# First w_gate group by units and both, fourth attention unit in single bursts, third weight groups by halves: a fused sliding-window attention and gated feed-forward kernel

## The chip, the cores and the metric

The kernel runs on one core of one Trainium2 chip. The metric is device time in microseconds (us) of one launch, the median of several runs.

## The reference

Attention over 8 batches x 8 heads, 576 positions of 64 numbers each, where a position sees itself and the 63 before it; then a feed-forward layer over the 4608 tokens, 512 numbers wide inside and out, 1536 wide in the middle.

```python
q, k, v: (8, 8, 576, 64) float32
scores = matmul(q, k^T) / sqrt(64);   masked where not 0 <= i - j < 64
attn   = softmax(scores);             x = matmul(attn, v)  -> (4608, 512)
out    = (maximum(x @ w_gate, 0) * (x @ w_val)) @ w_out       # float32, (4608, 512)
w_gate, w_val: (512, 1536);  w_out: (1536, 512)
```

## The kernel before

The tokens are worked on in tiles: four of 384 tokens (tile 0 to 3) and six of 512. The attention of a 384-token tile is done in two *units* of 192 tokens; units 0 and 1 belong to tile 0, units 2 and 3 to tile 1, and so on. The types on chip are 16-bit floats with 32-bit sums.

One unit goes through these steps, each a function of the kernel: `u_st` (scores on TensorE, 24 small products for each half of the heads, called `hh` 0 and 1), `u_exp` (ScalarE), `u_mask` (VectorE), `u_pv` (values on TensorE, again 24 small products for each `hh`), `u_recip` and `u_norm` (VectorE; `u_norm_act` does one half on ScalarE with six copies), and `u_turn` (two VectorE transpositions that write the x tile `xt`, two of its four chunks of 128 for each `hh`). Before a batch's first scores, q and k are loaded by POOL's DMA queue into `nats` (`qk_load`, L179) and transposed on VectorE (`qk_trans`, L199, two for k and two for q); v is loaded by `v_load` (L205) and spread by `v_spread` (L215 on an engine, L217 by SP's DMA queue).

The feed-forward layer has 12 output columns blocks `f` of 128 in its middle. Tiles 0 and 1 are computed by `hidden` (L589): for groups of four f, the products with w_gate (four chunks c of the contraction each), `relu` on ScalarE (L572), the products with w_val, and the gate product on VectorE (L575) that writes `g_sb`. Then `output` multiplies by w_out (L1023), copies the result on ScalarE and stores it by SP's queue (L1036). Later tiles use `fast_hidden` (L634; the sums on VectorE are L670), `fast_output`, and for the last six `SevenOut` (L847), which form fewer, larger products with prepared sums of the weights (`w_form`, L528) and of x (`x_form`). Nothing of these is changed but one list, `SEVEN[-1]`.

The weights come in by POOL's queue in three groups of four f for each matrix, and each group in two halves `a` of two contraction chunks each (`w_load`, L159). The order on POOL's queue is: v of units 0 and 1, first w_gate and w_val group, second groups, v of unit 2, third groups, q and k of the next batch, v of unit 3, w_out.

The order of instructions on every engine is written out by the program when it is built: the `Weaver` holds a clock and a list of planned steps with due times. The feed-forward products advance the clock by their assumed length, and steps that fall due are issued between them (`W.at(T, ...)`, `W.advance`). `w_need` makes the clock wait for a weight group's assumed landing. On the chip, semaphores alone decide: each engine runs its instructions in this order, each as soon as its operands are there. PSUM has eight banks; `one_bank` goes round banks 0 to 3 for the feed-forward products of tiles 0 and 1, `two_banks` round 4 to 7 for the attention units.

Of the kernel before, what the change touches and what calls it, by code (L numbers as in the profile page):

```python
# [10 lines left out]
FP32 = mybir.dt.float32  # L11
FP16 = mybir.dt.float16
# [35 lines left out]
def kernel(  # L48
# [10 lines left out]
    nc = tc.nc  # L59
# [94 lines left out]
    def w_load(wt, src, f0, f1, landed):  # L154

        if wt is not wo:
            ns = slice(128 * f0, 128 * f1)
            for a in range(2):
                nc.gpsimd.dma_start(wt[:, 2 * a:2 * a + 2, ns], src.rearrange("(a p e) n -> a p e n", a=2, e=2)[a, :, :, ns])  # L159
        if wt is wo:  # L160
            nc.gpsimd.dma_start(wo[:, f0:f1], src.rearrange("(c p) n -> p c n", p=128)[:, f0:f1])
        w_done.update(((wt.name, f), landed) for f in range(f0, f1))

    def w_need(wt, f):
        while (wt.name, f) not in w_done:
            W.pop()
        W.advance(w_done[wt.name, f])

# [176 lines left out]
    def u_recip(u, hhs=(0, 1)):  # L345
        d = units[u]
        if "r" not in d:
            d["r"] = a_n.tile([128, 2, SB, 1], FP32, name="r")
        for hh in hhs:
            nc.vector.reciprocal(d["r"][:, hh], pv_of(d, u, hh)[:, :, D:D + 1])  # L350
# [21 lines left out]
    def u_turn(u, hhs=(0, 1)):  # L372

        d = units[u]
        c0 = U * (u % 2)
        h0, h1 = hhs[0], hhs[-1] + 1
        for hh in range(h0, h1):
            dst = xt_tile(u // 2)[:, 2 * hh:2 * hh + 2, c0:c0 + U].rearrange("p e (s c) -> p s e c", c=32)
            nc.vector.transpose(dst, d["x"][:, hh])
# [27 lines left out]
    def part_written(banks):  # L407
        written.update((id(to), 0) for to in banks)
# [129 lines left out]
    def plan_exps(T, u, mask=True, gap=0.4, first=0.8):  # L538
        for i in range(G):
            W.at(T + first + gap * i, lambda i=i: u_exp(u, i))  # L540
            if mask:
                W.at(T + first + 0.45 + gap * i, lambda i=i: u_mask(u, i))
# [11 lines left out]
        while normed[0] < n:  # L554
            W.pop()

    def hidden(t, spans, f0=0, f1=NF, each=1):

        if t not in gs:
            gs[t] = g_sb_p.tile([128, NF, WT], FP16, name="g_sb"), {}  # L560
        g_sb, done = gs[t]
        xt = xt_tile(t)
        n = spans[0][1] - spans[0][0]

        w = 512 // n
# [12 lines left out]
        for fb in range(f0, f1, each):  # L578
            r2s = [f_sb.tile([128, 2, WT], FP32, name="pr", bufs=4) for _ in range(2)]
            r_sbs = {}  # L580
            for i, wt in enumerate((wg, wv)):
                for c0, f in ((c0, f) for c0, _ in spans for f in range(fb, fb + each, w)):
                    h = one_bank()
                    part_written([h])
                    for b in range(w):
                        W.advance(W.clock)
                        w_need(wt, f + b)
                        for c in range(NC):
                            nc.tensor.matmul(h[:, b * n:b * n + n], wt[:, c, (f + b) * 128:(f + b) * 128 + 128],  # L589
                                             xt[:, c, c0:c0 + n], start=(c == 0), stop=(c == NC - 1))  # L590
                        W.clock += 4 * (n + 7) / 2400.0
                    if i == 0:
                        r_sb = r_sbs[c0, f] = r2s[len(r_sbs) // 2][:, len(r_sbs) % 2]
                        W.at(W.clock, lambda r_sb=r_sb, h=h: relu(r_sb, h))
                    else:
                        W.at(W.clock, lambda f=f, c0=c0, r_sb=r_sbs[c0, f], h=h: gate(f, c0, r_sb, h))

    def fast_hidden(t, seven=None):

# [467 lines left out]
    XAT = -0.3  # L1067
    SEVEN_LAST = (("P6", "P5", "P2", "P7", "oP1", "P3", "P4"), ("P6", "P5", "P2", "P7", "oP1", "P4", "P3"))
    SEVEN = {n: ("P2", "v0", "v1", "P6", "P5a", "P7", "s0", "P5b", "P4", "s1", "P3") for n in (-5, -4, -3, -2)}
    SEVEN[-1] = ("v0", "P2", "P6", "v1", "P5a", "P7", "P5b", "P4", "h1", "P3")  # L1070

    SEVEN[0] = ("P2", "P4", "P5", "P6", "P7", "P3")

    with tc.manual_schedule():
# [45 lines left out]
        for hh in range(2):  # L1120
            u_recip(0, (hh,))
            u_norm(0, hh)
        u_turn(0)
        for hh in range(2):
            u_pv(1, (hh,), True)
        heat(1, units[1]["st"][3])
        for hh in range(2):
            u_recip(1, (hh,))
        u_norm_act(1, 1)
        u_norm(1, 0)  # L1130
        for hh in range(2):
            u_turn(1, (hh,))
# [16 lines left out]
        for u in (4, 5):  # L1149
            v_load(u)  # L1150
        for i, (name, hh) in enumerate((n, hh) for n in "kq" for hh in range(2)):
            W.at(31.6 + 1.4 * i, lambda name=name, hh=hh: qk_trans(1, name, hh))
        for hh, T in enumerate((36.6, 38.8)):
            W.at(T, lambda hh=hh: u_st(3, (hh,)))
            for i in range(G):
                W.at(T + 0.4 + 0.22 * i, lambda hh=hh, i=i: u_exp(3, i, (hh,)))
                W.at(T + 0.8 + 0.22 * i, lambda hh=hh, i=i: u_mask(3, i, (hh,)))
            W.at(T + 3.5 - 0.7 * hh, lambda hh=hh: u_pv(3, (hh,)))
            W.at(T + 4.0 - 0.7 * hh, lambda hh=hh: u_recip(3, (hh,)))
            W.at(T + 4.1 - 0.7 * hh, lambda hh=hh: u_norm(3, hh))  # L1160
            W.at(T + 4.6 - 0.7 * hh, lambda hh=hh: u_turn(3, (hh,)))
        W.at(37.4, lambda: v_spread(3, pool))
        W.at(40.6, lambda: behind_masks(3))

        def pair(t, TA, TB, P):
            for u, T in ((2 * t, TA), (2 * t + 1, TB)):
# [53 lines left out]
        def ahead(t):  # L1220
            T = W.clock
            long = widths[t] == WT
            ends = T + (32.7 if long else 22.5)
            if t + 2 <= LAST:
                qk_turns(t + 2, T, LATE if t - 1 in FAST_OUT else (0.1, 1.4, 8.0, 14.2) if long else (0.1, 1.4, 6.1, 10.7) if t < NS - 1 else (2.4, 6.1, 10.7, 14.2))
                v_ahead(t + 2, ends, ends + VAT if t in FAST_OUT else ends - 5.0 if long else T + 3.0 if t == 2 else ends + 1.5)
# [8 lines left out]
        for T, gap, eng, some in ((40.5, 0.1, nc.gpsimd, sums[0][:4] + sums[1][:3]), (52.8, 0.1, nc.gpsimd, sums[1][3:8]),  # L1235
                                  (48.2, 0.6, nc.vector, sums[0][4:8]), (68.1, 0.1, nc.gpsimd, sums[0][8:]),
                                  (64.5, 0.7, nc.vector, sums[1][8:])):
            for i, (w, j, n) in enumerate(some):
                W.at(T + gap * i, lambda eng=eng, w=w, j=j, n=n: w_form(eng, (wg, wv)[w], n, j))
# [21 lines left out]
        while any(id(one) in unread for one in singles[:4]):  # L1261
# [73 lines left out]
```

## Time and profile before

| what | value |
|---|---|
| time, median of 3 runs | 301.93 us (301.9 to 302.15) |
| profiled execution: its own time | 302.04 us |
| its span | 300.3 us |
| TensorE busy | 289.6 us, 96% |
| VectorE busy | 251.7 us, 84% |
| ScalarE busy | 196.0 us, 65% |
| POOL busy | 201.7 us, 67% |
| granted TensorE clock | 1.0 throughout |

PE is the page's name for TensorE's matrix products, DVE for VectorE, ACT for ScalarE, POOL for GpSimd, SP for the engine that issues most stores. A row of the timeline gives the start, the time to the end of the last instruction, the engine, the line, the operation, the tiles written and read with their form, the count, and in brackets the idle time of the engine before the row with what ended it. Products that follow each other overlap, so the spacing of their starts, not the length of one, is what a product costs.

### The profile page before, as it was taken

What the parts mean: (1) busy time and instruction counts of PE and PEld (TensorE: products, weight loads), DVE (VectorE), ACT (ScalarE), POOL (GpSimd) and SP (SyncE); (2) the same over time, 40 slices, a digit from 0 to 9 for tenths busy, and PEclk for the clock granted to TensorE, in tenths of its full rate; (3) what the DMA queues carried; (4) which work ended last, traced back from release to release, by engine and by line L of the source; (5) the groups of instructions that cost most, each with busy time, mean ns of one, the idle gap of its engine ahead of it and who ended that gap; (6) DMA issues with size and microseconds to landing.
All of it is one profiled execution on the core that took longest, in us unless ns stands there. A gap on an engine that the chain in (4) does not pass through costs nothing.

```text
span 300.3 us, 11073 instructions
## 1 busy us (share of the span) xinstructions
PE 289.6 (96%) x4643; PEld 239.4 (80%) x4643; DVE 251.7 (84%) x517; ACT 196.0 (65%) x408; POOL 201.7 (67%) x241
## 2 busy tenths in 40 slices
PE   4899999999999999999999999999999999999994
PEld 2475877748957975888888888888888888888894
DVE  5947895997995999789999899989858985896584
ACT  3545336258848848885798579857985698538850
POOL 8767689868957893985957595759375617441750
PEclk9999999999999999999999999999999999999999
DMA  7999999979919636911399239922911210031013
GB/s 216 183 196 194 194 197 179 160 131 241 80 40 181 164 70 149 146 42 38 61 219 120 60 53 219 126 57 53 173 37 35 74 41 0 3 103 41 0 38 105
DMA packets 59506, 33.20 MB, mean 111 GB/s; under 512 B 39552, under 2 KB 53824, under 8 KB 59456
## 3 DMA queue, kind: packets, MB, share of 16 engines
q0 software_dynamic: 46688, 18.29, 52.3%
q1 hardware_dynamic: 12192, 13.75, 15.1%
q8 instruction: 36, 0.59, 0.8%
q10 hardware_dynamic: 576, 0.46, 0.5%
q14 instruction: 14, 0.11, 0.1%
HBM read 37.75 MB, written 9.44 MB: 157 GB/s over the span
## 4 chain that ended last, share of the span: by engine, by line
PE 87%; DMA 5%; POOL 4%; DVE 2%; issue 1%; DVEq 0%; POOLq 0%
PE bank L634 46%; PE bank L847 17%; PE bank L589 7%; PE bank L767 5%; PE bank L1023 5%; PE bank L265 3%; DMA wg<-in_moe_w_gate_dram 3%; PE bank L465 2%; DMA v<-in_v_dram 2%; POOL v L205 1%; PE bank L336 1%; POOL wg L159 1%; DVE g_sb L659 1%; DVE g_sb L797 0%; POOL wv L159 0%
## 5 line engine op out<-in xcount | busy, mean ns | idle before, releaser
L659 POOL TENSOR_TENSOR g_sb<-pr 128x512 f16<-128x512 f32 (+1 forms) x36 | 42.7, 1193 | 43.6 <-ACT pr L676 43.6
L670 DVE TENSOR_TENSOR pr<-bank,pr 128x512 f32<-128x512 f32 (+1 forms) x96 | 58.5, 649 | 3.6 <-PE bank L634 1.9
L653 ACT COPY pr<-bank 128x512 f32<-128x512 f32 (+1 forms) x96 | 49.1, 566 | 13.7 <-PE bank L634 13.5
L659 DVE TENSOR_TENSOR g_sb<-r,bank 128x512 f16<-128x512 f32 (+1 forms) x48 | 31.3, 652 | 23.8 <-ACT r L703 22.4
L847 PEld LDWEIGHTS <-g_sb 128*128 128x128 f16 x444 | 41.8, 98 | 5.2 <-issue 0.2
L634 PE MATMUL bank<-xc,vs 128*128 128x256 f16 (+1 forms) x288 | 41.3, 266 | 0.0
L634 PE MATMUL bank<-xc,us 128*128 128x256 f16 (+1 forms) x288 | 41.3, 266 | 0.0
L634 PEld LDWEIGHTS <-vs 128*128 128x128 f16 x384 | 36.5, 98 | 3.5
L634 PEld LDWEIGHTS <-us 128*128 128x128 f16 x384 | 36.5, 98 | 3.3
L205 POOL DMA_DIRECT2D v<-in_v_dram x41 | 34.7, 866 | 2.2 <-DMA nats<-in_q_dram 1.0
L676 ACT ACTIVATE pr<-pr 128x512 f32<-128x512 f32 (+1 forms) x48 | 29.3, 610 | 9.8 <-DVE pr L670 9.8
L703 ACT ACTIVATE r<-bank 128x512 f32<-128x512 f32 (+1 forms) x48 | 27.7, 577 | 4.8 <-PE bank L634 4.0
L634 PEld LDWEIGHTS <-wg 128*128 128x128 f16 x288 | 27.4, 98 | 3.2
L634 PEld LDWEIGHTS <-wv 128*128 128x128 f16 x288 | 27.4, 98 | 2.6
L634 PE MATMUL bank<-xt,wg 128*128 128x256 f16 (+1 forms) x192 | 27.5, 266 | 0.0
L634 PE MATMUL bank<-xt,wv 128*128 128x256 f16 (+1 forms) x192 | 27.5, 266 | 0.0
L797 POOL TENSOR_TENSOR g_sb<-g_sb,xus 128x512 f16<-128x512 f16 x24 | 27.1, 1148 | 0.0
L847 PE MATMUL bank<-wo,g_sb 128*128 128x256 f16 (+1 forms) x222 | 26.6, 270 | 0.0
L430 ACT ACTIVATE pw<-bank 128x512 f16<-128x512 f32 x48 | 25.3, 605 | 1.1 <-PE bank L265 0.7
L847 PE MATMUL bank<-wts,g_sb 128*128 128x256 f16 (+1 forms) x222 | 25.4, 270 | 0.2 <-DVE xw L484 0.2
L643 ACT COPY bank<-bank 128x512 f32<-128x512 f32 (+1 forms) x48 | 24.6, 553 | 0.0
L572 ACT ACTIVATE pr<-bank 128x384 f32<-128x384 f32 x24 | 11.9, 501 | 15.5 <-PE bank L589 12.5
(107 smaller groups left out, 559.8 us busy)
## 6 DMA issues: line engine op xcount, KB each, us to landing
out_dram<-o_sb SPq DMA_DIRECT2D x30, 256.0 KB, 3.1
nats<-in_k_dram POOLq DMA_DIRECT2D x15, 288.0 KB, 6.1
nats<-in_q_dram POOLq DMA_DIRECT2D x15, 288.0 KB, 8.0
v<-in_v_dram POOLq DMA_DIRECT2D x31, 128.0 KB, 8.2
v<-v SPq DMA_DIRECT2D x27, 66.0 KB, 2.7
v<-v SPq DMA_DIRECT2D x13, 132.0 KB, 2.5
wg<-in_moe_w_gate_dram POOLq DMA_DIRECT2D x6, 256.0 KB, 6.4
wv<-in_moe_w_val_dram POOLq DMA_DIRECT2D x6, 256.0 KB, 8.1
```

Of the source, the lines that this page charges most:

```text
L205: nc.gpsimd.dma_start(v16s[b % 2][lo:hi, g, :, 0:64], v[b, :, 64 * g - 64 + lo:64 * g - 64 + hi].rearrange("h p d -> p h d"))
L430: nc.scalar.activation(d["p"][g].rearrange("p n c -> p (n c)"), d["st"][g], ACT.Exp, scale=scale)
L589: nc.tensor.matmul(h[:, b * n:b * n + n], wt[:, c, (f + b) * 128:(f + b) * 128 + 128], xt[:, c, c0:c0 + n], start=(c == 0), stop=(c == NC ...
L634: nc.tensor.matmul(to[:, HT * m:HT * m + HT], w[:, k, 128 * m:128 * m + 128], x[:, k], start=(first and m == 0 and k == 0), stop=(k == 1), ...
L643: nc.scalar.copy(at[j, "B", i][:, 0:TW], at[j, "A", i][:, 0:TW])
L653: nc.scalar.copy(pr[:, i], at[j, "A", i][:, 0:TW])
L659: eng.tensor_tensor(gh[:, f:f + 2, h], pair(r), pair(v), MUL)
L670: nc.vector.tensor_tensor(pr[:, i], to[:, 0:TW], pr[:, i], ADD)
L676: nc.scalar.activation(pr[:, 0], pr[:, 0], ACT.Relu)
L703: nc.scalar.activation(r, to[:, 0:TW], ACT.Relu)
L797: eng.tensor_tensor(to, x, y, op)
L847: nc.tensor.matmul(at[key][:, QN * m * whole:QN * m * whole + n1 - n0], A[:, 128 * m:128 * m + 128], B[:, c, n0:n1], start=(first and m == ...
```

## The change

- `w_need` and `w_done` know the two halves of a weight group, and the first half's assumed landing is 1.3 us before the second's.
- The first group of tile 0 is written out in `first_hidden`. Its four PSUM blocks hold: f 0 and 1 of unit 0; f 2 of both units; f 3 of both units; f 0 and 1 of unit 1. With w_gate, the first contraction half of f 0, 1 and 2 for unit 0 runs first, then the second half, then f 3 for both units at once (384 columns), then unit 1 of f 0, 1, and of f 2.
- In the rest of tile 0, `hidden` can run the first halves of several outputs before their second halves: three outputs for the third w_gate group, two for the third w_val group. One output of the second group (f 4) runs each product as two of 192 columns.
- Tile 1's first half takes its banks from a list that also has two of the attention's banks.
- Unit 1's reciprocals are split, and the one that `u_norm_act` needs goes between unit 0's transpositions.
- Unit 2's scores and values are planned earlier. Unit 3's scores are one burst of 48 products and its values another, where each was two of 24.
- `output(0)` computes all three row blocks before the second half of tile 1, where it computed two before and one after.
- Due times move: q and k transpositions of units 3 and 6, values of units 4 and 5, one group of weight sums, v loads of a later tile.
- In `SEVEN[-1]`, the first part of product P5 comes before the second half (`v1`) of the last tile's values.

```diff
-    def w_need(wt, f):
-        while (wt.name, f) not in w_done:
+        w_done.update(((wt.name, f, a), landed - 1.3 * (1 - a)) for f in range(f0, f1) for a in range(2))
+    def w_need(wt, f, a=1):
+        while (wt.name, f, a) not in w_done:
             W.pop()
...
-    def hidden(t, spans, f0=0, f1=NF, each=1):
+    def hidden(t, spans, f0=0, f1=NF, each=1, halves={}, split=(), banks=None):
...
+                first = halves.get((fb, i), 1)
+                for group in [items[:first]] + [[item] for item in items[first:]]:
+                    hs = [singles[banks.pop(0)] if banks else one_bank() for _ in group]
+                    part_written(hs)
+                    for cs in ((0, 1), (2, 3)) if len(group) > 1 else (range(NC),):
+                        for (c0, f), h in zip(group, hs):
+                            for b in range(w):
+                                W.advance(W.clock)
+                                w_need(wt, f + b, cs[-1] // 2)
+                                m = n // 2 if i == 0 and f in split else n
+                                for c, lo in ((c, lo) for c in cs for lo in range(0, n, m)):
+                                    nc.tensor.matmul(h[:, b * n + lo:b * n + lo + m], ...)
...
+    def first_hidden():
+        blocks = (((0, 0), (1, 0)), ((2, 0), (2, 1)), ((3, 0), (3, 1)), ((0, 1), (1, 1)))
+        STEPS = (
+            ((0, (0, 1), (0, 1), False), (1, (0, 1), (0,), False), (0, (2, 3), (0, 1), True), (1, (2, 3), (0,), False), (2, (0, 1), (0, 1), False), (2, (2, 3), (0, 1), True), (3, (0, 1, 2, 3), (0, 1), True), (1, (0, 1, 2, 3), (1,), True)),
+            ((0, (0, 1, 2, 3), (0, 1), True), (2, (0, 1, 2, 3), (0, 1), True), (3, (0, 1, 2, 3), (0, 1), True), (1, (0, 1, 2, 3), (0, 1), True)),
+        )
...
-    SEVEN[-1] = ("v0", "P2", "P6", "v1", "P5a", "P7", "P5b", "P4", "h1", "P3")
+    SEVEN[-1] = ("v0", "P2", "P6", "P5a", "v1", "P7", "P5b", "P4", "h1", "P3")
...
-        u_turn(0)
+        u_turn(0, (0,))
         for hh in range(2):
             u_pv(1, (hh,), True)
         heat(1, units[1]["st"][3])
-        for hh in range(2):
-            u_recip(1, (hh,))
+        u_recip(1, (1,))
         u_norm_act(1, 1)
+        u_turn(0, (1,))
+        u_recip(1, (0,))
         u_norm(1, 0)
...
-        W.at(23.2, lambda: u_st(2))
-        plan_exps(23.2, 2)
-        plan_values(27.4, 2)
+        W.at(22.0, lambda: u_st(2))
+        plan_exps(22.0, 2)
+        plan_values(25.9, 2)
...
-        for hh, T in enumerate((36.6, 38.8)):
-            W.at(T, lambda hh=hh: u_st(3, (hh,)))
...
-            W.at(T + 3.5 - 0.7 * hh, lambda hh=hh: u_pv(3, (hh,)))
...
+        W.at(37.9, lambda: u_st(3))
...
+        W.at(37.9 + 5.0, lambda: u_pv(3))
...
-        plan_batch(2, (36.5, 36.6, 42.5, 42.6), (52.0, 53.6, 56.9, 57.1))
+        plan_batch(2, (36.5, 36.6, 42.5, 42.6), (52.0, 52.9, 56.9, 57.1))
...
-        pair(2, 46.6, 50.0, 54.0)
+        pair(2, 46.6, 50.0, 55.7)
...
-        hidden(0, ((0, U), (U, TT)), 0, 4, 4)
-        hidden(0, ((0, TT),), 4, NF, 4)
-        hidden(1, ((0, U),), each=4)
-        output(0, (0, 1), (0, 8, NF))
+        first_hidden()
+        hidden(0, ((0, TT),), 4, NF, 4, split=(4,), halves={(8, 0): 3, (8, 1): 2})
+        hidden(1, ((0, U),), each=4, banks=[0, 1, 4, 5, 2, 3, 0, 1, 2, 3, 0, 1])
+        taken["one"] += 2
+        output(0, (0, 1, 2), (0, 4, 8, NF))
         ready(1)
         hidden(1, ((U, TT),), each=4)
-        output(0, (2,))
         output(1)
```

More of the change, by code (lines that the diff above doesn't have):

```diff
@@ L581, in hidden @@
             for i, wt in enumerate((wg, wv)):
[L582 to L596, printed above, removed]
+                items = [(c0, f) for c0, _ in spans for f in range(fb, fb + each, w)]
@@ new lines, in first_hidden, with products, relu, gate @@
+    def first_hidden():
+        g_sb, done = gs[0] = g_sb_p.tile([128, NF, WT], FP16, name="g_sb"), {}
+        xt = xt_tile(0)
+        r2s = [f_sb.tile([128, 2, WT], FP32, name="pr", bufs=4) for _ in range(2)]
+        r_sbs = [r2s[n // 2][:, n % 2, 0:TT] for n in range(4)]
+        blocks = (((0, 0), (1, 0)), ((2, 0), (2, 1)), ((3, 0), (3, 1)), ((0, 1), (1, 1)))
+        parts = lambda tile: tile.rearrange("p (w n) -> p w n", w=2)
+        STEPS = (
+            ((0, (0, 1), (0, 1), False), (1, (0, 1), (0,), False), (0, (2, 3), (0, 1), True), (1, (2, 3), (0,), False), (2, (0, 1), (0, 1), False), (2, (2, 3), (0, 1), True), (3, (0, 1, 2, 3), (0, 1), True), (1, (0, 1, 2, 3), (1,), True)),
+            ((0, (0, 1, 2, 3), (0, 1), True), (2, (0, 1, 2, 3), (0, 1), True), (3, (0, 1, 2, 3), (0, 1), True), (1, (0, 1, 2, 3), (0, 1), True)),
+        )
+        def products(h, i, n, cs, us=(0, 1), more=False):
+            wt = (wg, wv)[i]
+            block = blocks[n]
+            W.advance(W.clock)
+            w_need(wt, block[-1][0], cs[-1] // 2)
+            whole = i == 0 and n == 2
+            for c in cs if whole else ():
+                f = block[0][0]
+                nc.tensor.matmul(h[:, 0:TT], wt[:, c, f * 128:f * 128 + 128], xt[:, c, 0:TT],
+                                 start=(c == 0), stop=(c == NC - 1), skip_group_check=True)
+            for m in () if whole else us:
+                f, u = block[m]
+                for c in cs:
+                    nc.tensor.matmul(h[:, U * m:U * m + U], wt[:, c, f * 128:f * 128 + 128], xt[:, c, U * u:U * u + U],
+                                     start=(c == 0 and m == us[0] and not more), stop=(c == NC - 1), skip_group_check=True)
+            W.clock += len(us) * len(cs) * (U + 7) / 2400.0
+        def relu(n, h):
+            nc.scalar.activation(r_sbs[n], h[:, 0:TT], ACT.Relu)
+        def gate(n, h):
+            (f, u), (f1, u1) = blocks[n]
+            if f == f1:
+                to = g_sb[:, f:f + 1, 0:TT]
+                nc.vector.tensor_tensor(to, r_sbs[n].rearrange("p (w n) -> p w n", w=1), h[:, 0:TT].rearrange("p (w n) -> p w n", w=1), MUL)
+                done[f] = TT
+            else:
+                nc.vector.tensor_tensor(g_sb[:, f:f + 2, U * u:U * u + U], parts(r_sbs[n]), parts(h[:, 0:TT]), MUL)
+                done.update({f: U * u + U, f1: U * u + U})
+        for i, then in enumerate((relu, gate)):
+            hs = {}
+            for n, cs, us, ends in STEPS[i]:
+                more = n in hs
+                if not more:
+                    hs[n] = one_bank()
+                    part_written([hs[n]])
+                products(hs[n], i, n, cs, us, more and 0 not in us)
+                if ends:
+                    W.at(W.clock, lambda n=n, h=hs[n], then=then: then(n, h))
```

35 lines of the change are left out of this document (23 added, 12 removed).

## The prediction

> **What bounds the kernel now.** I read the page's head, then the timeline of TensorE, and then those of the engines that end its waits. From the head:
>
> ```profile
> span 300.3 us, 11073 instructions
> PE 289.6 (96%) x4643; PEld 239.4 (80%) x4643; DVE 251.7 (84%) x517; ACT 196.0 (65%) x408; POOL 201.7 (67%) x241
> ```
>
> TensorE is busy for 96% of the span, so only its few waits and its overheads can be won. The waits of the first feed-forward tile that the change is about stand in the timeline (start, length, count, in brackets the idle time before the row and what ended it):
>
> ```profile
> 16.50 1.48 PE L589 MATMUL bank<-xt,wg 128*128 128x192 f16 x16 [0.66 <-DVE xt L379]
> 17.82 2.80 PE L589 MATMUL bank<-xt,wv 128*128 128x192 f16 x32
> 20.45 2.76 PE L589 MATMUL bank<-xt,wg 128*128 128x384 f16 x16
> ...
> 26.24 0.49 PE L589 MATMUL bank<-xt,wg 128*128 128x384 f16 x2
> 27.09 0.50 PE L589 MATMUL bank<-xt,wg 128*128 128x384 f16 x2 [0.36 <-DMA wg<-in_moe_w_gate_dram]
> ...
> 29.97 2.76 PE L589 MATMUL bank<-xt,wv 128*128 128x384 f16 x16
> 32.57 1.48 PE L589 MATMUL bank<-xt,wg 128*128 128x192 f16 x16
> ```
>
> A 192-column product takes 0.082 us (2.63 us for 32, from 17.82 to 20.45), a 384-column one 0.163 (2.60 for 16, from 29.97 to 32.57). So two products from 26.24 would have ended at 26.57, and the restart at 27.09 says that 0.52 us is lost there, more than the bracket's 0.36. From 28 us on the timeline has no bracket on TensorE except one near the end, shown below. What the change takes out before that, it keeps only if no other engine becomes late.
>
> **Part 1: the first group.** Here the wait of 0.66, for the second unit's half of the x tile, is the one that ends last. What makes that half:
>
> ```profile
> 13.22 1.03 DVE L379 STREAM_TRANSPOSE xt<-xus 128x384 f16<-128x384 f16 x2
> 14.17 0.23 DVE L350 RECIPROCAL r<-bank 128x6 f32<-128x6 f32 x2
> ...
> 14.95 0.58 DVE L379 STREAM_TRANSPOSE xt<-xus 128x384 f16<-128x384 f16 x1
> 15.80 0.58 DVE L379 STREAM_TRANSPOSE xt<-xus 128x384 f16<-128x384 f16 x1 [0.27 <-ACT xus L369]
> 14.43 1.34 ACT L369 ACTIVATE xus<-bank,r 128x64 f16<-128x64 f32 x6 [1.60 <-DVE r L350]
> ```
>
> The last transposition ends at 16.38 and waits 0.27 us for ScalarE's six copies. The change puts the reciprocal that ScalarE needs between the first two transpositions, so its copies start near 14.0 instead of 14.43, end near 15.3, and hold nobody. VectorE's own chain then runs through: two transpositions take 0.95 (13.22 to 14.17), so one follows the other by 0.48; the last but one starts at 14.95, plus 0.10 because the norm now waits for the reciprocal just ahead of it; the last starts 0.48 later and takes 0.58. That is 14.95 + 0.10 + 0.48 + 0.58 = 16.11: **0.27 us earlier**. The new order of products wins nothing more. After the last x half come two 384-column products and twelve of 192 (1.31 us), where before there were sixteen of 192 (1.32); the waits only change places among the earlier ones. The split of one output of the second group gives eight products of 0.082 for four of 0.163: nothing. Bounds: 0, if the copies still end last, and 0.4. What is late next is the first w_val group:
>
> ```profile
> L159 POOL DMA_DIRECT2D wv<-in_moe_w_val_dram x2: 698/704/710, 8.8 to 9.5; - x2
> DMA to landing us min/median/max: 7.6/7.8/8.0
> ```
>
> Its second half lands at 9.5 + 8.0 = 17.5; products start at 17.82 - 0.27 = 17.55 and want it 0.16 later. It fits.
>
> **Part 2: the third groups by halves.** Issue and time to landing of the third w_gate and w_val groups:
>
> ```profile
> L159 POOL DMA_DIRECT2D wg<-in_moe_w_gate_dram x2: 707/708/710, 17.3 to 18.0; - x2
> DMA to landing us min/median/max: 8.5/8.8/9.0
> ```
>
> ```profile
> L159 POOL DMA_DIRECT2D wv<-in_moe_w_val_dram x2: 698/704/710, 19.1 to 20.3; - x2
> DMA to landing us min/median/max: 9.3/9.3/9.3
> ```
>
> So w_gate lands at 25.8 and 27.0, w_val at 28.4 and 29.6. Nothing ahead of these on POOL's queue is changed. The third group is reached at 26.24 - 0.27 = 25.97. Now the values of unit 2 (0.49 us) come first, then six products of the first half (0.98): the second half is wanted at 27.44, after 27.0. The 0.52 is gone and the 0.27 kept, **0.79 in all**: w_val starts at 29.18, wants its second half after four products at 29.83, and it is there at 29.6. Late next are the values themselves. They need unit 2's masks and POOL's copies of v:
>
> ```profile
> 24.10 1.70 POOL L215 COPY v<-v 64x512 f16<-64x512 f16 x2 [3.05 <-DMA v<-in_v_dram]
> 25.03 1.25 DVE L306 TENSOR_TENSOR p<-p,mask 128x384 f16<-128x384 f16 x2
> ```
>
> The copies end at 25.80, before 25.97. The scores move 1 us ahead, so that the four masks lie under the copies; at 0.6 each, as in this row, the last ends near 25.9. I take 0, bounds 0 and 0.4.
>
> **Part 3: one burst each for unit 3.** Its scores and its values ran as two bursts of 24 small products each. What a burst costs:
>
> ```profile
> 38.32 0.82 PE L589 MATMUL bank<-xt,wg 128*128 128x192 f16 x8
> 39.08 0.36 PE L265 MATMUL bank<-qT,kT 32*128 32x64 f16 x24
> 39.37 0.83 PE L589 MATMUL bank<-xt,wg 128*128 128x192 f16 x8
> ...
> 50.67 0.55 PE L265 MATMUL bank<-qT,kT 32*128 32x64 f16 x48
> 51.16 1.49 PE L589 MATMUL bank<-xt,wg 128*128 128x192 f16 x16
> ```
>
> Eight products from 38.32 end at 38.98, but the burst starts at 39.08: 0.10. A burst of 24 takes 0.29, one of 48 takes 0.49, so 0.09 is fixed. Two bursts less save 2 x 0.19 = **0.38 us**. Against that, the burst of scores now needs all four transpositions of q and k, where the first half needed two. VectorE has the same six gate products and three transpositions ahead of the last one as before, and starts them 0.79 earlier, so it should end near 37.8; TensorE arrives at 32.57 - 0.79 + 9 x 0.66 = 37.7. I take 0.1 lost, bounds 0 and 0.4. The third row block of the first output, 12 products, moves ahead of the second half of tile 1, so unit 3's x half gets more cover, not less.
>
> **Part 4: VectorE behind it, around 57 to 75 us.** Here I expect to give some back. The change lets the values of units 4 and 5 be planned later and the four transpositions of the next q and k earlier. In VectorE's new order the two q transpositions stand right behind the first norm of unit 4, ahead of its second norm, its turns and all of unit 5. Their loads:
>
> ```profile
> L179 POOL DMA_DIRECT2D nats<-in_q_dram x2: 538/554/571, 49.7 to 50.3; - x2
> DMA to landing us min/median/max: 7.8/8.4/9.0
> ```
>
> ```profile
> 57.06 1.02 DVE L357 TENSOR_TENSOR xus<-bank,r 128x384 f16<-128x384 f32 x2
> ...
> 60.00 2.31 DVE L199 STREAM_TRANSPOSE qT<-nats 128x576 f32<-128x576 f32 x2
> 62.16 0.54 DVE L357 TENSOR_TENSOR xus<-bank,r 128x384 f16<-128x384 f32 x1
> ...
> 72.22 0.56 DVE L659 TENSOR_TENSOR g_sb<-r,bank 128x384 f16<-128x384 f32 x1 [1.00 <-PE bank L634]
> 72.76 1.02 DVE L670 TENSOR_TENSOR pr<-bank,pr 128x384 f32<-128x384 f32 x2
> ```
>
> The second q half lands at 50.3 + 9.0 = 59.3. Before, VectorE came to it after 60 and did not wait. Now it comes at about 58 and waits. From there: one transposition (1.08) to 60.4; the work that was moved behind (57.53 to 60.00: 2.47); then what stood between 62.16 and 71.22, where the idle 1.00 begins: 9.06. So the gate product at 72.22 comes at 71.9, only 0.3 earlier, while TensorE comes 0.79 + 0.38 - 0.1 = 1.07 earlier. The sums of 72.76 shift likewise, and TensorE needs them:
>
> ```profile
> 73.70 0.49 PE L634 MATMUL bank<-xt,us 128*128 128x192 f16 x4
> 74.03 0.49 PE L634 MATMUL bank<-xt,vs 128*128 128x192 f16 x4
> ```
>
> The first sum ends at 72.76 + 0.54 = 73.30, 0.40 before it is used, the second at 73.78, 0.25 before. Late by 0.75 less a cover of 0.25: TensorE stands for about **0.5 us** in the third tile. Bounds: 0 if the loads, issued up to 0.4 sooner because POOL's waits for unit 3's masks end sooner, land so, and 1.5 if they land 1 us later. After these rows the brackets in VectorE's queue let it catch up, and it is not late again.
>
> **Part 5: near the end** P5a goes ahead of the second half of the last tile's values:
>
> ```profile
> 262.72 0.69 PE L465 MATMUL bank<-v,pw 128*32 128x65 f16 x64
> 263.59 4.09 PE L847 MATMUL bank<-wts,g_sb 128*128 128x256 f16 x36 [0.18 <-DVE xw L484]
> ```
>
> The 0.18 is P5a's wait for a bank that the norm of the first half frees. In the new order P5a takes a bank that is long free, and the values need the late one only for their last eight products, some 0.9 us later. **0.2 us** won; bounds 0 and 0.25.
>
> **The sum**: 0.27 + 0.52 + 0.38 - 0.1 - 0.5 + 0.2 = 0.77 us. Against the profiled execution (302.04, of which 300.3 is the span) that is 301.27; the median of the runs, 301.93, lies 0.11 lower, so 301.16, say **301.2**. What a measurement of this kernel can tell from no change is 0.2%, 0.6 us: the forecast is only just beyond it.
>
> **Rivals.** *Nothing given back* (0.24): the q loads land early, VectorE keeps step, and Part 4 costs 0 to 0.1: 300.7. For it speaks the earlier issue; against it that VectorE is without a bracket from 57.06 to 71.22.
>
> *All given back* (0.20): the change stores three row blocks of the first output from about 48.4 on, where two were stored:
>
> ```profile
> L1036 SPq DMA_DIRECT2D out_dram<-o_sb x2: 441/560/679, 49.3 to 50.1; - x2
> DMA to landing us min/median/max: 3.8/6.2/8.5
> ```
>
> The second store took 8.5 us beside the q loads, so they share the engines. If the third store's 256 KB push the second q half by 0.6 us, Part 4 costs 1.1 and the time is 301.8. The Trainium skill's page "DMA: Bandwidth & Descriptors" (Queues, rings and completion order) has each DMA engine go round between the queues that have work, a packet at a time; by that rule a longer queue on SP delays the q loads only while both hold work. It has work in both kernels until 58.6, so the rule makes the delay small; no run here shows it yet.
>
> *Slower* (0.08): the same q load, much later. Each 0.1 us of its landing costs TensorE 0.1. The gain is gone when it lands 0.8 us later, at 60.1, and the kernel is measurably slower from 60.7 on; a full extra store at the quicker one's 3.8 us would put it at 63.1 and the time near 304. Against it: the store is queued behind two others, and most of it should run after the loads.
>
> *The halves don't bite* (0.05): products wait for a whole group. Against it, the row at 26.24 shows two products of the first half running ahead of the wait. Then 0.5 less: 301.7.
>
> **Chances.** The forecast's own case (0.43) spans 300.9 to 301.6, some three quarters of it beyond 0.2%. With the first rival that makes faster by over 0.2%: 0.6; within 0.2%: 0.3; slower: 0.1. The range that leaves two in ten out is 300.4 to 302.1.
>
> **What would show it.** Right: no wait of TensorE for w_gate after 25 us, w_val's third group starting near 29.2, the third tile (69.08 before) starting near 68.0, a VectorE bracket that ends with the q load near 59, a TensorE bracket near 72 that ends with pr, none near 263. Wrong: a TensorE wait for unit 3's q transposition or masks over 0.4 us, or one for a gate product of VectorE between 53 and 65.

## The result and the profile after

| | before | after |
|---|---|---|
| time, median of 22 runs each | 301.9 us (301.6 to 302.7) | 301.34 us (300.78 to 302.52) |
| ratio after to before, 95% interval | | 0.9979 (0.9972 to 0.9986) |
| profiled execution: own time, span | 302.04, 300.3 us | 301.49, 299.8 us |
| TensorE / VectorE busy | 289.6 / 251.7 us | 290.2 / 252.2 us |

The change makes the kernel 0.63 us faster (0.42 to 0.85). The forecast was 301.2. The sum came out, but its largest terms did not, as the runs below show.

TensorE's waits after the change (what it did, what it waited for, us in total, times, longest):

```profile
PE bank L232 <- DVE bias L129: 4.4, 1, 4.4
PE bank L627 <- DVE xt L379: 0.6, 1, 0.6
PE bank L336 <- ACT p L299: 0.2, 1, 0.2
PE bank L465 <- issue: 0.2, 1, 0.2
```

The first is at the start of the kernel, before any of the work that was changed. The waits for w_gate and, near the end, for xw are gone. The timeline of TensorE (start, length, form, count, bracket for idle time):

```profile
15.93 0.94 PE L627 MATMUL bank<-xt,wg 128*128 128x384 f16 x4 [0.63 <-DVE xt L379]
...
17.74 2.93 PE L632 MATMUL bank<-xt,wv 128*128 128x192 f16 x32
20.51 2.12 PE L594 MATMUL bank<-xt,wg 128*128 128x192 f16 x16
...
26.40 0.56 PE L336 MATMUL bank<-v,p 128*32 128x65 f16 x48
26.89 2.77 PE L594 MATMUL bank<-xt,wg 128*128 128x384 f16 x16
29.50 2.76 PE L594 MATMUL bank<-xt,wv 128*128 128x384 f16 x16
32.10 1.48 PE L594 MATMUL bank<-xt,wg 128*128 128x192 f16 x16
...
38.14 0.75 PE L265 MATMUL bank<-qT,kT 32*128 32x64 f16 x48
38.82 0.83 PE L594 MATMUL bank<-xt,wg 128*128 128x192 f16 x8
...
56.05 1.25 PE L336 MATMUL bank<-v,p 128*32 128x65 f16 x96
...
59.55 3.62 PE L1085 MATMUL bank<-wo,g_sb 128*128 128x512 f16 x16
...
68.49 0.49 PE L696 MATMUL bank<-xt,wg 128*128 128x192 f16 x4
```

- The first w_val group starts at 17.74, only 0.08 earlier than before (17.82), and its 32 products now take 2.77 (17.74 to 20.51) where they took 2.63. One of them waits 0.13 for the activation that frees its bank.
- The third w_gate group runs through, and tile 1 starts at 32.10 instead of 32.57.
- Unit 3's scores take 0.68 (38.14 to 38.82) where a burst of 48 took 0.49: they wait 0.2 for the last q transposition.
- The values of units 4 and 5 take 1.25 where the same row was 1.06 before.
- The third tile starts at 68.49 instead of 69.08.

VectorE did not fall behind around 57 to 72 us, where the prediction had it wait:

```profile
57.54 2.33 DVE L199 STREAM_TRANSPOSE qT<-nats 128x576 f32<-128x576 f32 x2
...
71.63 0.56 DVE L721 TENSOR_TENSOR g_sb<-r,bank 128x384 f16<-128x384 f32 x1 [0.41 <-PE bank L696]
```

```profile
L179 POOL DMA_DIRECT2D nats<-in_q_dram x2: 538/554/571, 49.4 to 49.9; - x2
DMA to landing us min/median/max: 6.0/6.9/7.9
```

The second q half landed at 49.9 + 7.9 = 57.8, ahead of its transposition at 58.6, and at 71.63 VectorE is the one that waits.

### The profile page after: what moved, and what is told of

Read it like the earlier page. It is cut to its first block, busy times and chain, and to the rows that moved or that the text cites. A ratio compares the mean times of both kernels' runs of the same rounds, so it can differ in the third digit from the quotient of the medians.

```text
span 299.8 us, 11066 instructions
## 1 busy us (share of the span) xinstructions
PE 290.2 (97%) x4643; PEld 239.7 (80%) x4643; DVE 252.2 (84%) x513; ACT 195.7 (65%) x404; POOL 201.9 (67%) x241
## 3 DMA queue, kind: packets, MB, share of 16 engines
HBM read 37.75 MB, written 9.44 MB: 157 GB/s over the span
## 4 chain that ended last, share of the span: by engine, by line
PE 93%; DVE 2%; DMA 2%; POOL 1%; issue 1%; DVEq 0%; POOLq 0%
PE bank L696 46%; PE bank L909 18%; PE bank L594 9%; PE bank L829 5%; PE bank L1085 5%; PE bank L265 3%; PE bank L465 3%; DMA v<-in_v_dram 2%; PE bank L632 1%; PE bank L336 1%; DVE xt L379 1%; DVE xus L357 1%; POOL nats L179 0%; DVE v L215 0%; PE bank L627 0%
## 5 line engine op out<-in xcount | busy, mean ns | idle before, releaser
L909 PE MATMUL bank<-wo,g_sb 128*128 128x256 f16 (+1 forms) x222 | 26.6, 270 | 0.0
L299 ACT ACTIVATE p<-bank 128x384 f16<-128x384 f32 (+1 forms) x40 | 14.1, 442 | 10.3 <-PE bank L265 10.1
```

The source lines that it names most:

```text
L909: nc.tensor.matmul(at[key][:, QN * m * whole:QN * m * whole + n1 - n0], A[:, 128 * m:128 * m + 128], B[:, c, n0:n1], start=(first and m == ...
```

## The experiments

Each kernel is compared with the kernel before on its own chip; the ratios and the places of the trace that matter stand in one table. "Landing" is that of the second half of the third w_gate group, "tile 1" and "third tile" are the starts of their first products, "between" is their distance.

| kernel | median, us | ratio to before (95%) | landing | tile 1 | third tile | between |
|---|---|---|---|---|---|---|
| before | 301.9 | 1 | 27.05 | 32.57 | 69.08 | 36.51 |
| before_again | 301.76 | (one run) | 26.84 | 32.38 | 68.89 | 36.51 |
| after | 301.34 | 0.9979 (0.9972 to 0.9986) | 27.04 | 32.10 | 68.49 | 36.39 |
| no_halves | 301.26 | 0.9981 (0.9972 to 0.9990) | 26.81 | 32.35 | 68.56 | 36.21 |
| values_late | 302.32 | 1.0012 (0.9991 to 1.0033) | 26.73 | 32.81 | 69.56 | 36.75 |
| neither | 301.17 | 0.9970 (0.9959 to 0.9981) | 27.16 | 32.69 | 68.71 | 36.02 |
| banks | 301.11 | 0.9970 (0.9959 to 0.9981) | 26.80 | 32.40 | 68.43 | 36.03 |
| only_3_5 | 300.95 | 0.9976 (0.9957 to 0.9995) | 26.64 | 32.30 | 68.32 | 36.02 |
| front_back | 300.95 | 0.9974 (0.9964 to 0.9983) | 26.52 | 32.58 | 68.59 | 36.01 |
| tail_back | 301.38 | 0.9990 (0.9981 to 0.9999) | 26.53 | 32.42 | 68.62 | 36.20 |
| more_bursts | 302.72 | 1.0031 (1.0016 to 1.0047) | 26.22 | 32.47 | 70.22 | 37.75 |
| turns_early | 301.31 | 0.9982 (0.9973 to 0.9990) | 26.70 | 32.35 | 68.37 | 36.02 |
| best | 300.90 | 0.9973 (0.9961 to 0.9985) | 26.98 | 32.74 | 68.75 | 36.01 |
| q_late | 303.36 | 1.0061 (1.0039 to 1.0083) | 27.11 | 32.59 | 70.63 | 38.04 |

### Does the third weight group carry the gain?

Three kernels take Part 2 apart. no_halves:

```diff
-        hidden(0, ((0, TT),), 4, NF, 4, split=(4,), halves={(8, 0): 3, (8, 1): 2})
+        hidden(0, ((0, TT),), 4, NF, 4, split=(4,))
-        w_load(*G3[2], 27.0)
+        w_load(*G3[2], 26.0)
```

The second line only keeps the program's clock from moving later steps.

> The third weight groups' products run whole outputs again; unit 2's scores and values stay where the change put them. Theory 1 (the halves pay): the wait for w_gate near 27 us comes back, 0.3 to 0.5, and the kernel takes 301.6 to 301.8. Theory 2 (the values placed ahead are cover enough): the group starts at 26.89 and wants its second half after two products of 0.163, at 27.22; that half landed at 27.04, so there is no wait, and the time is that of the changed kernel, 301.3 within 0.2.

values_late:

```diff
-        W.at(22.0, lambda: u_st(2))
-        plan_exps(22.0, 2)
-        plan_values(25.9, 2)
+        W.at(23.2, lambda: u_st(2))
+        plan_exps(23.2, 2)
+        plan_values(27.4, 2)
```

> Unit 2's scores and values are planned at their old times (23.2 and 27.4); the third groups keep their halves. Theory 1 (each of the two edits carries a part of the 0.5): about 0.2 to 0.3 slower than the changed kernel, 301.6. Theory 2 (either alone covers it): the group starts at 26.40, six products of the first half last to 27.38, the second half landed at 27.04, so no wait and 301.3 within 0.2. The values may show a wait of their own here or lose the one for the masks; the prediction put that at 0.

neither has both edits:

> Both are undone: whole outputs in the third groups and unit 2 at its old times. If either edit alone is enough, this is the only one of the three in which the wait is back: the second half is wanted at 26.40 + 0.33 = 26.73 and lands at 27.04, so 0.3 us of wait and 301.6 to 301.7 in all; with a restart as long as in the kernel before (0.52 lost for a bracket of 0.36) it is 0.45 and 301.8. If the gain of the changed kernel comes from elsewhere (the order of the first group, the single bursts), this stays at 301.3.

Theory 2 held for no_halves: no wait for w_gate, and the time of the changed kernel. Its only new wait there is one of 0.25 for unit 2's masks; the values, 0.49 long when nothing holds them, take 0.73 to the next row:

```profile
26.41 0.80 PE L336 MATMUL bank<-v,p 128*32 128x65 f16 x48
27.14 2.77 PE L594 MATMUL bank<-xt,wg 128*128 128x384 f16 x16
```

values_late missed both expectations: it is slower than the changed kernel by some 1 us. The halves without the early values make a new wait:

```profile
27.67 0.81 PE L594 MATMUL bank<-xt,wg 128*128 128x384 f16 x4 [0.52 <-DVE g_sb L575]
...
57.72 0.65 PE L336 MATMUL bank<-v,p 128*32 128x65 f16 x56 [0.66 <-issue]
```

```profile
25.11 1.05 DVE L306 TENSOR_TENSOR p<-p,mask 128x384 f16<-128x384 f16 x2
...
26.54 0.61 DVE L306 TENSOR_TENSOR p<-p,mask 128x384 f16<-128x384 f16 x2
27.08 1.01 DVE L575 TENSOR_TENSOR g_sb<-pr,bank 128x384 f16<-128x384 f32 x2
```

With halves, TensorE asks for the third output's bank after four products instead of eight. The gate product that frees it starts at 27.08, behind four masks that stand late on VectorE. So the two edits of Part 2 are not two gains: as this profile has it, the halves need the early values. The other 0.66, which costs 0.73 here, has nothing to do with the halves: TensorE waits for its next instructions (last section). How much of the 1 us in the times is the one and how much the other isn't settled.

neither was the surprise. It lacks both edits and is as fast as the changed kernel. In its profile only 0.1 is lost to w_gate, with TensorE 0.5 later from the start (its last product ahead of the first group starts at 14.18, in the changed kernel at 13.67) and the group nearly in. So the 0.52 that the prediction took from the profile of before is not a fixed loss.

### What do parts 1 and 2 win together?

front_back undoes the first group alone (`first_hidden()` becomes `hidden(0, ((0, U), (U, TT)), 0, 4, 4)` again, and the reciprocals and transpositions of unit 1 stand as before):

```diff
-        first_hidden()
+        hidden(0, ((0, U), (U, TT)), 0, 4, 4)
...
-        u_turn(0, (0,))
+        u_turn(0)
...
-        u_recip(1, (1,))
+        for hh in range(2):
+            u_recip(1, (hh,))
         u_norm_act(1, 1)
-        u_turn(0, (1,))
-        u_recip(1, (0,))
```

> The first group's products and the order of its transpositions and reciprocals are those of the kernel before; the rest is the changed kernel. The prediction's term: 0.27 slower, 301.6. The reading of the two traces: w_val starts 0.08 later (17.82 for 17.74) but does not wait 0.13 for an activation, so the next group starts where it did, and the time is 301.3 within 0.15.

only_3_5 joins the edits of neither and front_back and drops `split=(4,)`. TensorE's order up to 36 us is then that of the kernel before, but for unit 2's values, which come after eight products of the third w_gate group where they came after four. The second half of the group is wanted by the third product in both. The order of the row blocks, the bank list and the moved due times stay as the change has them.

> Only the single bursts of unit 3 (with what the plan moves for them) and the swap near the end are left of the change; the first group and the third groups are as in the kernel before. Theory 1 (what parts 1 and 2 win is lost again at the q transposition that ends at 38.5, and a late start of TensorE makes the w_gate wait vanish by itself): 0.49 of burst overhead and 0.25 at the end against the kernel before, 301.2 to 301.4, no slower than the changed kernel by more than 0.1. Theory 2 (the prediction's sum, in which parts 1 and 2 carry 0.79): 0.5 to 0.8 slower than the changed kernel, 301.85 to 302.1.

before_again is the kernel before, profiled a second time.

> The kernel before, profiled once more. If the 0.52 at 26.6 is a fixed loss, the wait for w_gate's third group is there again with 0.3 to 0.5. If it depends on when that group lands and when TensorE starts, as the kernel with the two last parts alone suggests (the same order up to 38 us, landing at 26.64, no wait), it can be anything from 0 to 0.5, and the third tile then starts up to 0.5 earlier than 69.08.

Theory 1 held as to the time: only_3_5 has neither part 1 nor part 2 and is 0.24% faster than the kernel before, the changed kernel 0.21%. front_back, 0.26% faster, is no slower for the lack of part 1. The interval of only_3_5 is wide and would by itself leave room for a few tenths; that of neither leaves none for the 0.52, that of front_back hardly any for the 0.27. Of theory 1's two reasons, though, only the second is seen. Nothing is lost at 38.5 in only_3_5. What differs from the profile of before is the wait that isn't there; the eight products from 26.51 take 1.40 to the values at 27.91, which is 8 x 0.163 and the 0.10 ahead of a burst:

```profile
26.51 1.46 PE L594 MATMUL bank<-xt,wg 128*128 128x384 f16 x8
27.91 0.56 PE L336 MATMUL bank<-v,p 128*32 128x65 f16 x48
```

```profile
L159 POOL DMA_DIRECT2D wg<-in_moe_w_gate_dram x2: 707/708/710, 17.4 to 18.1; - x2
DMA to landing us min/median/max: 8.0/8.2/8.5
```

The second half lands at 26.6 and not at 27.0. The kernel before itself, profiled again, has no wait there either (four products from 26.59 to the values at 27.33, 0.74 with the 0.10 ahead of a burst):

```profile
26.59 0.81 PE L589 MATMUL bank<-xt,wg 128*128 128x384 f16 x4
27.33 0.56 PE L336 MATMUL bank<-v,p 128*32 128x65 f16 x48
```

Over the fourteen profiles the landing goes from 26.22 to 27.16, and the start of tile 1 from 32.10 to 32.81, with no order between kernels that have parts 1 and 2 and those that have not: 32.10, 32.42, 32.47, 32.35 and 32.59 (after, tail_back, more_bursts, turns_early, q_late) against 32.57, 32.38 and 32.30 (before twice, only_3_5). The changed kernel's own profile is the earliest of all, so the pair of profiles shown above flatters this part.

### Banks, and the transpositions of q

banks adds one line in `first_hidden`, at the start of the w_val group, so that its outputs take the banks in the order in which the activations free them:

```diff
             hs = {}
+            if i == 1:
+                singles[1:4] = singles[2], singles[3], singles[1]
```

> In the first group the w_val outputs take their banks in the order in which the first activations free them. Theory 1: the changed kernel loses 0.13 us at 18.4 us because its second w_val output takes the bank whose activation comes last; here the 32 products from 17.74 last 2.63 instead of 2.77 and the kernel is 0.1 to 0.15 faster, 301.2. Theory 2: something that ends later takes it back (the next w_gate group then starts at 20.4 and wants weights, which landed by then; unit 2's masks at 26.3): the products get faster there but unit 2's values wait, and the time is 301.3.

turns_early:

```diff
-            W.at((32.0, 33.4, 34.8, 36.2)[i], lambda name=name, hh=hh: qk_trans(1, name, hh))
+            W.at((31.0, 32.4, 33.8, 35.2)[i], lambda name=name, hh=hh: qk_trans(1, name, hh))
```

> The four transpositions of the second batch's k and q are planned 1.0 us earlier: the first k half ahead of a gate product, the first q half right behind the second k half, the last q half still behind the gate products of the next group. If the last q transposition is what swallows an early TensorE at 38.5, it now ends near 37.8, the 0.2 at 38.3 is gone and the kernel is 0.1 to 0.2 faster than the changed one, 301.15. Rival (VectorE as a whole is late there, and any other order moves the wait to a gate product): a wait for a gate product appears between 33 and 40 and the time is 301.3 or more.

best has both:

> The earlier transpositions together with the banks in order of release. If both waits were real losses, 0.13 and 0.2: 301.0, and TensorE reaches the third tile near 68.2. If something outside TensorE's order sets the time when it reaches 38 us (the landing of the third w_gate group, between 26.2 and 27.2 in the profiles so far, and unit 2's masks), there is nothing to win beyond the kernel with the two last parts of the change alone: 301.1 to 301.3, third tile at 68.3 to 68.5.

In banks the w_val group takes 2.64 again, so the 0.13 did come from the bank; but unit 2's values now take 0.70, so they wait 0.21 for the masks, and in this profile nothing is kept:

```profile
17.96 2.80 PE L632 MATMUL bank<-xt,wv 128*128 128x192 f16 x32
20.60 2.12 PE L594 MATMUL bank<-xt,wg 128*128 128x192 f16 x16
...
26.49 0.77 PE L336 MATMUL bank<-v,p 128*32 128x65 f16 x48
27.19 2.77 PE L594 MATMUL bank<-xt,wg 128*128 128x384 f16 x16
```

In turns_early the last q transposition ends at 38.1 (37.03 and about 1.1), and the scores run without the wait:

```profile
38.39 0.55 PE L265 MATMUL bank<-qT,kT 32*128 32x64 f16 x48
38.87 0.83 PE L594 MATMUL bank<-xt,wg 128*128 128x192 f16 x8
```

```profile
37.03 1.23 DVE L199 STREAM_TRANSPOSE qT<-nats 128x576 f32<-128x576 f32 x1
```

"Between" falls from 36.21 (no_halves, which also starts tile 1 at 32.35) to 36.02. So the wait is real and worth 0.2 where it occurs. It is a race too: in five kernels without this edit (values_late, neither, banks, only_3_5 and front_back) these scores take 0.48 to 0.50 as well. In time neither kernel is told from the changed one: their intervals overlap its own. The same holds for best, 0.27% faster than before; I don't call it an improvement.

### The price of a burst

more_bursts splits the scores of units 4 to 7:

```diff
-                W.at(T, lambda u=u: u_st(u))
+                W.at(T, lambda u=u: u_st(u, (0,)))
+                W.at(T + 0.9, lambda u=u: u_st(u, (1,)))
```

> The scores of units 4 to 7 run as two bursts of 24 each instead of one of 48: four bursts more. If a burst costs a fixed 0.10 ahead and 0.09 inside whatever stands beside it: 4 x 0.19 = 0.76 slower than the changed kernel, 302.1, and the tile that started at 68.49 starts at about 69.2. Rival (the fixed part is hidden when TensorE is ahead of VectorE, as the qT wait at 38.5 suggests): 0.3 or less, 301.5.

It is 0.5% slower than the changed kernel, 1.6 us by the ratios and so twice what was expected. The stretch with units 6 and 7, whose scores now begin with 24 products, has nothing else in it:

```profile
60.86 3.62 PE L1085 MATMUL bank<-wo,g_sb 128*128 128x512 f16 x16
64.41 0.36 PE L265 MATMUL bank<-qT,kT 32*128 32x64 f16 x24
```

From 60.86 to the third tile at 70.22 are 9.36, in the changed kernel 8.94 (59.55 to 68.49): 0.21 for each burst more. The Trainium skill's page "TensorEngine Tiling (Array Packing)" (Tiling Modes) says that a change of tiling mode drains TensorE; it gives no price. The 0.21 here is the price of a whole burst, of which that drain can be a part. So the price per burst held, and what came on top lies in the stretch before: 0.2 for a gate product at 55.3 and 0.4 around an idle bracket of 0.33 at the values of units 4 and 5 (the changed kernel loses 0.2 there), which is a wait for instructions (last section). Whether the split bursts bring that time with them isn't settled.

### The end of the kernel

tail_back:

```diff
-    SEVEN[-1] = ("v0", "P2", "P6", "P5a", "v1", "P7", "P5b", "P4", "h1", "P3")
+    SEVEN[-1] = ("v0", "P2", "P6", "v1", "P5a", "P7", "P5b", "P4", "h1", "P3")
```

> Only the swap of P5a and the second half of the last tile's values is undone. The prediction's term: the wait for xw near 263 is back with 0.2, and the kernel is 0.2 to 0.25 slower than the changed one, 301.55. Rival (something else bounds the end, such as the last stores): the wait is back and the time is 301.3.

The wait is back, first in tail_back, then the same place in the changed kernel:

```profile
262.15 0.69 PE L465 MATMUL bank<-v,pw 128*32 128x65 f16 x64
263.02 3.22 PE L909 MATMUL bank<-wts,g_sb 128*128 128x256 f16 x28 [0.18 <-DVE xw L484]
```

```profile
262.83 0.69 PE L465 MATMUL bank<-v,pw 128*32 128x65 f16 x64
263.45 2.79 PE L909 MATMUL bank<-wts,g_sb 128*128 128x256 f16 x24
```

From the values to the next product are 0.87 and 0.62, so 0.25; by the ratios 0.3 us, with intervals that overlap. The term is confirmed by its place in the trace, and its size in time is no more than bounded.

### Does a late q load cost what the prediction said?

q_late puts the two q loads of the next batch behind three v loads on POOL's queue:

```diff
-        plan_batch(2, (36.5, 36.6, 42.5, 42.6), (52.0, 52.9, 56.9, 57.1))
+        plan_batch(2, (36.5, 36.6, 42.75, 42.76), (52.0, 52.9, 56.9, 57.1))
```

> On POOL's queue the two loads of the next q move behind three loads of v, 2.7 us later; nothing else moves. The prediction's mechanism (each 0.1 us of the second half's landing costs TensorE 0.1): landing near 61 instead of 57.8 is 3.2 later; less the 0.8 by which it now lands ahead of its transposition at 58.6, the idle 0.41 at 71.6 and the cover of 0.25, 1.7 to 1.9 slower, 303.1. Rival (VectorE has enough idle time between 62 and 75, or TensorE has other work to go on with): within 0.3 of the changed kernel.

```profile
59.58 1.26 DVE L199 STREAM_TRANSPOSE qT<-nats 128x576 f32<-128x576 f32 x1 [1.47 <-DMA nats<-in_q_dram]
61.03 1.26 DVE L199 STREAM_TRANSPOSE qT<-nats 128x576 f32<-128x576 f32 x1 [0.19 <-DMA nats<-in_q_dram]
```

```profile
64.33 0.18 PE L265 MATMUL bank<-qT,kT 32*128 32x64 f16 x1 [0.73 <-DVE xus L357]
65.25 0.52 PE L265 MATMUL bank<-qT,kT 32*128 32x64 f16 x45 [0.74 <-DVE xus L357]
...
70.63 0.49 PE L696 MATMUL bank<-xt,wg 128*128 128x192 f16 x4
```

The mechanism is there. The load lands at 61.0, and "between" is 38.04. Of the 2.02 above the 36.02 of a kernel without a wait, 0.20 is the wait for unit 3's q transposition, which this profile has as well (its scores at 38.62 take 0.68); so the late load costs 1.8 us, which was expected. If each 0.1 of the landing costs 0.1, as the prediction has it, the cost begins at 59.2; the prediction's working puts that point at 58.8. One landing can't show the slope itself. The place was wrong. TensorE stands at 64 us, where unit 6's scores want the banks that the norms of units 4 and 5 have still to read, not at 72 with the sums. In best the second half landed at 59.04 and cost nothing ("between" 36.01), which agrees with 59.2.

## Why the prediction was right, and where it was not

**The total** was right (301.2 forecast, 301.34 measured), but by luck: two errors cancel. The 0.79 entered as won at the front doesn't show in the times, and neither does the 0.5 entered as lost behind.

**Part 1 (0.27 won).** The first step, that the wait of 0.66 for the second unit's half of the x tile "is the one that ends last", doesn't hold for the products that it was read from. In the second profile of the kernel before, the same product starts at 16.77, while the last transposition still runs (16.37 to 16.95):

```profile
16.77 1.55 PE L589 MATMUL bank<-xt,wg 128*128 128x192 f16 x16 [0.58 <-issue]
```

It needs only the transposition before that, and waits for its instructions (last section). So did the product at 16.50 in the first profile, whose transposition had ended at 15.53; the x tile was complete at 16.38, but the product that needs its last part, two behind, started only at 16.66. Some 0.2 of the loss there had nothing to do with the x tile. In front_back it starts at 17.03, 0.7 after the x tile is complete, so the times, not that profile, price this part.

The step "VectorE's own chain then runs through" failed too. The x tile is complete at 16.34, not 16.11 (16.38 before; counted from the heat product just ahead of the group, 2.67 after it in place of 2.78):

```profile
13.94 0.20 DVE L350 RECIPROCAL r<-bank 128x6 f32<-128x6 f32 x1
14.05 0.54 DVE L379 STREAM_TRANSPOSE xt<-xus 128x384 f16<-128x384 f16 x1
...
15.30 1.04 DVE L379 STREAM_TRANSPOSE xt<-xus 128x384 f16<-128x384 f16 x2
```

The reciprocal that was moved ahead waits for unit 1's second half of values and holds the second transposition back to 14.05. And the prediction, which said "The new order of products wins nothing more", did not look at what the new order does to the banks: 0.13 are lost at the second w_val output. The time shows no gain from this part (front_back).

**Part 2 (0.52 won, 0.27 kept).** The step that failed is "0.52 us is lost there", read as a loss of every run. It is the outcome of a race between a landing that moves by 0.9 us and a start that moves by 0.6 (the heat product that precedes the first group starts at 13.57 to 14.19 over the profiles). The kernel before lost 0.52 in one profile and nothing in the next, where TensorE was 0.44 later from the heat product on. The halves do what they say, but what they save is seldom there to be saved, and an early TensorE meets unit 2's masks (0.2 to 0.35) or the q transposition (0.2) next. The first was taken as 0 with bounds 0 and 0.4; it lay within them.

**Part 3 (0.38 less 0.1).** Right in kind, and the larger half of the real gain. Without a wait "between" is 36.02 where it was 36.51: 0.49. Some 0.05 of this is a wait for a gate product behind a score burst (0.34 from 36.66 to 37.00, where the other burst of 24 took 0.29); the rest fits two bursts at 0.21. The wait for q is 0 or 0.2, against 0.1 taken and bounds of 0 to 0.4.

**Part 4 (0.5 lost).** The mechanism was right, the point from which a late landing costs was 0.4 too early, and the landing was not as late. "The second q half lands at 50.3 + 9.0 = 59.3" took one landing as given. In the second profile of the kernel before:

```profile
L179 POOL DMA_DIRECT2D nats<-in_q_dram x2: 536/552/568, 49.5 to 50.1; - x2
DMA to landing us min/median/max: 5.5/5.9/6.3
```

That is 56.4, 2.9 earlier with the same program. The latest landings of this half, q_late aside, are 59.25, 59.04 and 57.83, and the cost begins at some 59.2. So Part 4 should have been 0 with a small chance of a tenth or two. The rival "all given back" needed the third store to push the load back. In the changed kernel three stores were issued from 49.3 on and the load came at 57.8 all the same. The Trainium skill's page "DMA: Bandwidth & Descriptors" (Queues, rings and completion order) has each DMA engine go round between the queues that have work. The prediction took from this that the delay is small, and the changed kernel agrees: its load took 7.9 beside three stores, where it took 9.0 beside two. The scatter of the landings is too large to show a delay of tenths.

**Part 5 (0.2 won).** Right: 0.25 at its place.

So what the runs support is 0.49 for the single bursts and 0.25 at the end, 0.74 together, less 0 to 0.2 at the q transposition; the measured 0.63 lies there. The rival "the halves don't bite" was nearer to the truth than its 0.05, but for another reason than it gave. "Nothing given back" was right about VectorE.

Of the signs named, the absent waits for w_gate and near 263 were seen, and w_val's third group came at 29.50, not 29.2. The third tile came at 68.49, not 68.0. The brackets near 59 and 72 were not there.

## What to carry to other kernels

A wait for a DMA in one profile is one draw: before it is entered as a gain, profile the same kernel again and see how far the landing and the waiting engine's start move against each other. Fixed costs on the bounding engine, such as a burst of another form, came out the same in every profile here and are the safer gain. An edit that makes one engine early should be followed to the next thing that this engine needs (a bank, a mask, a transposition), and two edits that remove the same wait must not be added.

## What the runs showed that was not expected

- Landings of the same load in the same program differ by almost 3 us (56.4 and 59.25 for the second q half), with issues only 0.2 apart. In the quicker case the two stores beside the load had been issued 1.4 earlier (47.9 and 48.7 instead of 49.3 and 50.1) and had landed by 53.0 instead of 58.6. That goes with the earlier landing; no run tests whether it makes it.
- TensorE waits for its own instructions. Brackets that name "issue" (the profile shows nothing that the engine waited for) stand inside long bursts of values: 0.66 at 57 us in values_late, 0.33 there in more_bursts, and in the changed kernel 0.1 there and 0.18 at 230.9 us:

```profile
231.09 0.22 PE L465 MATMUL bank<-v,pw 128*32 128x65 f16 x5 [0.18 <-issue]
```

Counting the restart, each costs 0.2 to 0.7. Counted from the start of the program, the products that stand are always the same ones: the 864th and the 3807th, and in the first tile the 224th, which is the one at 16.50 and 16.77 above. The first two are 23 x 128 - 1 products apart, and the 224th is 5 x 128 ahead of the 864th. The page has a DMA queue that brings instructions:

```profile
q8 instruction: 36, 0.59, 0.8%
```

That is 36 packets for 4643 products and their weight loads, 129 of each to a packet. So the products that stand fit the first ones of a new packet. In the traces they start 1.2 to 1.6 us after the end of their packet, and no product at such a border starts sooner in any of the fourteen profiles. In values_late the packet for the 864th ran from 55.23 to 56.13, and TensorE went on at 57.72; in the kernel called neither, where TensorE doesn't stand, it ran from 53.62 to 54.60, ahead of the need. That TensorE waits for it is read from these times: no run moved a packet, and why it comes late in some executions stays open. values_late and more_bursts also have the widest spread of times (301.3 to 305.5 and 301.9 to 304.7).
